# First MoE, chunks 2 to 8: high-weight products on high and low rows at once, halves added by DVE

## The chip, the cores and the metric

The kernel runs on one core of a Trainium2 chip. The metric is device time in microseconds of one execution. Its engines are PE (matrix products), PEld (PE's weight loads, shown apart), DVE (vector), ACT (scalar), POOL and SP (which issues loads).

## The reference

Three stages follow one another. Masked attention over 4 batches of 576 rows with 8 heads of 64 gives 2304 rows of 512. The first MoE normalises each row and adds a two-layer product:

```
xn = (x - mu) / np.sqrt(var + 1e-06) * g_ln
ch = np.maximum(xn @ w_ch1, 0.0) @ w_ch2     # w_ch1 512x2048, w_ch2 2048x512, fp32
return x + ch
```

The second MoE routes each row to one of 8 experts of hidden width 1024, again with a Relu between two products, and scales by the gate's probability.

## The kernel before, in words

Rows are worked in 9 chunks of CT = 256, numbered 0 to 8, kept transposed (model dimension on partitions). Every fp32 product is made of three products of a faster type: a value is split into a high part and the low rest, and high x high, high x low and low x high are summed in PSUM. `ln_split` (lines 620, 621) makes the split rows xc of a chunk: `xc[:, 0]` high (ACT), `xc[:, 1]` low (DVE), each 4 pieces of 256 columns. `w1t[f // 2]` holds the first weights with high at index 0 and low at index 1.

A tile is (c, f): chunk c and hidden block f of 128 units, 16 blocks to a chunk. `mm1(c, f)` sums 12 matmuls of 256 columns (4 pieces d by three terms) in the first half of a PSUM tile `ps_h`, of which there are two (tag "m"):

```
terms = [(d, a, b_) for d in range(4) for a, b_ in ((0, 0), (0, 1), (1, 0))]
for i, (d, a, b_) in enumerate(terms):
    pe.matmul(ps, w[:, a, d, o:o + 128], xcs[c][:, b_, d, :], ...)
act.activation(h[:, 0, :], ps, AF.Relu)
dve.scalar_tensor_tensor(h[:, 1, :], ps, 0.0, f32(h[:, 0, :]), op0=ALU.max, op1=ALU.subtract)
```

So ACT makes the high part of h (line 639, Relu), then DVE its low part (line 640). `mm2(c, f)` (line 653) multiplies h by the second weights, 12 matmuls into two PSUM tiles `acc` that sum over the 16 blocks. Its first matmul reads h's high part, its second the low part. `post` (lines 657, 658) then scales by the row's factor and adds to x.

The main loop walks over the tiles in `order`: chunks 0 and 1 interleaved, then chunks 2 to 8 block by block. At each it emits mm1 of this tile, and then mm2 of the tile before (`products`); at block 0 of a chunk from 2 on, the last block's mm2 comes first, ahead of the new chunk's mm1. Between them it emits side work: attention of batches 1 to 3 (lines 280 to 411, spread up to chunk 5), the next chunk's LayerNorm (lines 523 to 626), the routing of the chunk before (lines 673 to 764: `rt_rows` reads its products `ps_x` with ACT at line 675 and DVE at lines 676 and 677; the scans are at lines 717 and 718), and in chunk 8 the split of the first expert's weights (ACT line 780, DVE line 783) and its first rows (lines 873 to 897).

Each engine runs its instructions in one fixed order. That order isn't the source's: in this part the planner that builds the program takes, for each engine, whatever it models as ready at that time, the earliest in the source first, with durations of its own model. Waits between engines are put in by it as well. The pool `ln_p` holds one buffer of each tag.

Of the kernel before, what the change touches and what calls it, by code (L numbers as in the profile page):

```python
# [9 lines left out]
F32 = mybir.dt.float32  # L10
# [6 lines left out]
ALU = mybir.AluOpType  # L17
# [11 lines left out]
CT = 256  # L29
NCHUNK = NT // CT  # L30
# [27 lines left out]
ORDER = "TBXAMONF"  # L58

KA, NSURE = 4, 14  # L60


SMALL = 64
# [9 lines left out]
def attention_moe_moe(ctx: ExitStack, tc: tile.TileContext, q, k, v, g_ln, w_ch1, w_ch2, w_gate, w_local, w1, w2, out):  # L73
# [15 lines left out]
    pe, act, dve = Pin(nc.tensor), Pin(nc.scalar), Pin(nc.vector)  # L89
    pool, sp = nc.gpsimd, nc.sync  # L90

    def f32(ap):
        return ap.bitcast(F32)
# [19 lines left out]
    for j in range(2):  # L113
        m = mask_loc[64 * j:64 * j + 64, :]
        pool.affine_select(out=m, in_=m, pattern=[[-1, 128]], compare_op=ALU.is_ge, fill=-NEG, base=STR, channel_multiplier=1)
        pool.affine_select(out=m, in_=m, pattern=[[1, 128]], compare_op=ALU.is_ge, fill=-NEG, base=-1, channel_multiplier=-1)
        m = mask_str[64 * j:64 * j + 64]
# [35 lines left out]
    ln_p = ctx.enter_context(tc.tile_pool(name="ln_p", bufs=1))  # L153
    rt_p = ctx.enter_context(tc.tile_pool(name="rt_p", bufs=1))
    ps_acc = ctx.enter_context(tc.tile_pool(name="ps_acc", bufs=1, space=PSUM))
    ps_m = ctx.enter_context(tc.tile_pool(name="ps_m", bufs=2, space=PSUM))
# [22 lines left out]
    def side_r(shape, name):  # L179
        return ps_s["r"].tile(shape, F32, tag="s", name=name)  # L180
# [337 lines left out]
    lns, mus, xcs = {}, {}, {}  # L518
# [110 lines left out]

    def mm1(c, f):  # L630
        w, o = w1t[f // 2], (f % 2) * 128
        ps = ps_m.tile([128, 512], F32, tag="m", name="ps_h")[:, 0:CT]
        terms = [(d, a, b_) for d in range(4) for a, b_ in ((0, 0), (0, 1), (1, 0))]
        if c == 0:
            terms.sort(key=lambda t: t[1])
        for i, (d, a, b_) in enumerate(terms):
            pe.matmul(ps, w[:, a, d, o:o + 128], xcs[c][:, b_, d, :], start=(i == 0), stop=(i == 11))  # L637
        h = h_p.tile([128, 2, CT], F32R, tag="h", name="h")
        act.activation(h[:, 0, :], ps, AF.Relu)  # L639
        dve.scalar_tensor_tensor(h[:, 1, :], ps, 0.0, f32(h[:, 0, :]), op0=ALU.max, op1=ALU.subtract)  # L640
        hs[c, f] = h
# [322 lines left out]
    for n in range(2):  # L964
        i = n * (NE + 129)
# [97 lines left out]
    for t, (c, f) in enumerate(order):  # L1063
# [3 lines left out]
        if f == 0 and c > 1:  # L1067
# [6 lines left out]
            elif c == NCHUNK - 1:  # L1074
                load_turn(0)
                m2_p = ctx.enter_context(tc.tile_pool(name="m2_p", bufs=1))
        mm1(c, f)
        while late:
            post(late.pop(), 1)
# [31 lines left out]
    c = NCHUNK - 1  # L1111
# [39 lines left out]
    ps = side_r([1, 2, NE], "ps_n")  # L1151
# [86 lines left out]
    ps = side_r([128, NTILE], "ps_li")  # L1238
# [372 lines left out]
```

## Time and profile before

| what | value |
|---|---|
| median of 3 runs | 879.38 us (879.37 to 880.01) |
| profiled execution | 880.44 us, span 878.7 us |
| mean granted clock of PE | 0.992 |
| busy: PE, PEld, DVE, ACT, POOL | 850.7, 755.2, 470.5, 354.1, 152.4 us |
| first MoE, chunks 2 to 8 | about 195 to 604 us of the span |

Times in the rows below are from the span's start. Matmuls are pipelined: the duration of one is longer than the distance to the next one's start, and a merged row's length is from the first start to the last end. Idle time is what an engine stood still ahead of an instruction, with what released it.

### The profile page before, as it was taken

How to read it: one execution, taken by the hardware profiler on the slowest of the kernel's cores; microseconds unless marked ns; L12 is line 12 of the kernel's file. 1: busy time of each engine (PE TensorE's matmuls, PEld its weight loads, DVE VectorE, ACT ScalarE, POOL GpSimd, SP SyncE). 2: the span in 40 equal slices, each digit the busy share in tenths (PEclk: the TensorE clock that was granted, in tenths of full speed). 3: DMA queues.
4: the chain of work that ended last, by engine and by line, in shares of the span. 5: the costliest groups of instructions: out<-in, count | busy, mean ns of one | idle time of the engine just before them, and what ended most of it. 6: DMA issues, size and time to landing. Idle time of an engine off the chain costs nothing. (4 is left out here: it accounts for less than half of the span.)

```text
span 878.7 us, 18791 instructions
## 1 busy us (share of the span) xinstructions
PE 850.7 (97%) x7130; PEld 755.2 (86%) x7130; DVE 470.5 (54%) x1542; ACT 354.1 (40%) x857; POOL 152.4 (17%) x161
## 2 busy tenths in 40 slices
PE   9999899999999999999999999999989999999995
PEld 5678788889999999899999999999778877778774
DVE  4877766648666546655555464585824251121641
ACT  3687877642454233354221222242112252232651
POOL 2123332221120120120111212010031221111101
PEclk9999999999999999999999999999999999999998
DMA  9935342311212102210000000501265266445740
GB/s 182 264 116 182 110 143 45 89 38 52 67 41 47 49 2 55 53 37 20 25 1 25 1 26 1 193 29 47 92 226 203 94 225 249 144 146 210 268 150 23
DMA packets 96545, 87.15 MB, mean 99 GB/s; under 512 B 67378, under 2 KB 75574, under 8 KB 96440
## 3 DMA queue, kind: packets, MB, share of 16 engines
q1 hardware_dynamic: 89256, 69.61, 26.2%
q0 software_dynamic: 3552, 11.11, 3.8%
q10 hardware_dynamic: 3632, 5.09, 1.6%
q8 instruction: 59, 0.97, 0.5%
q14 instruction: 46, 0.38, 0.1%
HBM read 76.27 MB, written 9.97 MB: 98 GB/s over the span
## 5 line engine op out<-in xcount | busy, mean ns | idle before, releaser
L653 PE MATMUL acc<-h,w 128*128 128x256 f32 x1728 | 245.7, 290 | 3.4 <-DVE h L640 1.9
L637 PE MATMUL ps_h<-xc,w 128*128 128x256 f32 x1728 | 237.2, 286 | 0.1
L653 PEld LDWEIGHTS acc<-h,w 128*128 128x128 f32 x1728 | 218.3, 191 | 9.6 <-DVE h L640 3.6
L637 PEld LDWEIGHTS ps_h<-xc,w 128*128 128x128 f32 x1728 | 219.3, 192 | 2.2 <-DVE xc L621 0.5
L639 ACT ACTIVATE h<-ps_h 128x256 fp32r<-128x256 f32 x144 | 55.7, 388 | 214.6 <-PE ps_h L637 200.7
L640 DVE SCALAR_TENSOR_TENSOR h<-ps_h,h 128x256 fp32r<-128x256 f32 x144 | 60.6, 421 | 98.9 <-ACT h L639 98.4
L87 PE MATMUL ps_y<-wx,ht 128*128 128x512 f32 x336 | 83.6, 398 | 0.0
L87 PE MATMUL ps_h<-wx,xs 128*128 128x512 f32 x336 | 81.0, 397 | 0.0
L87 PEld LDWEIGHTS ps_h<-wx,xs 128*128 128x128 f32 x336 | 62.7, 188 | 14.8
L87 PEld LDWEIGHTS ps_y<-wx,ht 128*128 128x128 f32 x336 | 61.1, 188 | 11.9 <-issue 0.2
L482 POOL TENSOR_TENSOR w<-stg,w 128x512 fp32r<-128x512 f32 x32 | 44.0, 1374 | 125.6 <-ACT w L481 76.5
L1462 DVE TENSOR_TENSOR ht<-ps_th,ht 128x512 fp32r<-128x512 f32 x28 | 18.2, 686 | 39.4 <-ACT ht L1461 39.1
L1448 ACT ACTIVATE h<-ps_h 128x512 f32<-128x512 f32 x28 | 15.2, 595 | 57.8 <-PE ps_h L87 57.8
L783 DVE TENSOR_TENSOR wx<-raw,wx 128x1024 fp32r<-128x1024 f32 x32 | 37.3, 1220 | 1.3 <-ACT wx L780 1.3
L461 ACT ACTIVATE stg<-stg 128x512 f16<-128x512 f32 x27 | 37.2, 1377 | 0.0
L780 ACT CAST wx<-raw 128x1024 fp32r<-128x1024 f32 x32 | 31.8, 1057 | 5.7 <-PE acc L653 4.1
L355 ACT ACTIVATE sm<-sm,st 128x54 f32<-128x54 f32 (+1 forms) x80 | 27.6, 347 | 13.2 <-DVE st L343 13.2
L1486 POOL DMA_INDIRECT out_dram<-y,idx x14 | 18.5, 1323 | 77.5 <-ACT y L1485 57.9
L1461 ACT CAST ht<-ps_th 128x512 fp32r<-128x512 f32 x28 | 15.1, 589 | 35.6 <-PE ps_th L87 35.6
L1124 PE MATMUL ps_h2t<-x,wx 128*128 128x256 f32 x192 | 26.7, 297 | 2.7 <-DVE h2t L1129 2.7
L1124 PEld LDWEIGHTS ps_h2t<-x,wx 128*128 128x128 f32 x192 | 25.1, 202 | 3.1 <-DVE h2t L1129 2.9
L1485 ACT ACTIVATE y<-ps_y,pr 128x512 f32<-128x512 f32 x18 | 12.4, 688 | 34.2 <-PE ps_y L1475 16.8
(397 smaller groups left out, 1178.7 us busy)
## 6 DMA issues: line engine op xcount, KB each, us to landing
raws<-in_moe_w_dram SPq DMA_DIRECT2D x20, 1024.0 KB
stg<-in_moe_w_ch_dram SPq DMA_DIRECT2D x32, 512.0 KB
raw<-in_moe_w_dram SPq DMA_DIRECT2D x16, 1024.0 KB
xrows<-row ACTq DMA_DIRECT2D x9, 520.0 KB
qnat<-in_q_dram SPq DMA_DIRECT2D x48, 72.0 KB
knat<-in_k_dram SPq DMA_DIRECT2D x48, 72.0 KB
v<-in_v_dram SPq DMA_DIRECT2D x24, 72.0 KB
v<-in_v_dram SPq DMA_DIRECT2D x72, 18.0 KB
```

Source lines behind the costliest of these rows:

```text
L87: return lambda *args, **kw: tc.keep_in_program_order(fn(*args, **kw))
L355: act.activation(sm[0:m, i, :], (ps if mode else sm)[0:m, i, :], AF.Exp, bias=st[0:m, 0, i:i + 1], scale=-1.0, **({} if mode else dict(acc ...
L461: keep(act.activation(t.bitcast(F16)[..., 1], f32(t[..., 1]), AF.Copy, scale=2.0 ** -112))
L482: keep(pool.tensor_tensor(w[:, 1], r, f32(w[:, 0]), op=ALU.subtract))
L637: pe.matmul(ps, w[:, a, d, o:o + 128], xcs[c][:, b_, d, :], start=(i == 0), stop=(i == 11))
L639: act.activation(h[:, 0, :], ps, AF.Relu)
L640: dve.scalar_tensor_tensor(h[:, 1, :], ps, 0.0, f32(h[:, 0, :]), op0=ALU.max, op1=ALU.subtract)
L653: pe.matmul(accs[c][d // 2][:, d % 2, :], w[:, a, f % 2, d * 128:(d + 1) * 128], h[:, b_, :], start=(f == 0 and (a, b_) == (0, 0) and d % ...
L780: act.copy(wx[i][:, 0, :], raw[i // 2][:, i % 2, :])
L783: dve.tensor_tensor(wx[i][:, 1, :], raw[i // 2][:, i % 2, :], f32(wx[i][:, 0, :]), op=ALU.subtract)
L1124: pe.matmul(ps[:, j, :], wx[d][:, b_, 128 * f:128 * f + 128], x[:, a, d, :], start=(d == 0 and (a, b_) == PASS[0]), stop=(d == 3 and (a, b ...
L1486: pool.indirect_dma_start(out=out, out_offset=bass.IndirectOffsetOnAxis(ap=places(s)[1], axis=0), in_=y, in_offset=None, bounds_check=NT - ...
```

## The change

In chunks 2 to 8 mm1 uses the whole PSUM tile of 512 columns. Four matmuls take a high weight piece as stationary operand and the high and the low rows of that piece as one moving operand of 512 columns: the first 256 columns of the PSUM tile then hold high x high, the last 256 high x low. Four matmuls of 256 columns add low x high to the first half. ACT copies the second half to a new SBUF tile `low` (tag "low" in `ln_p`), DVE adds it to the first half in PSUM, and the Relu and the low half go on from there as before. Chunks 0 and 1 stay as they were.

```
+BOTH = range(2, NCHUNK)
     def mm1(c, f):
         w, o = w1t[f // 2], (f % 2) * 128
-        ps = ps_m.tile([128, 512], F32, tag="m", name="ps_h")[:, 0:CT]
+        ps = ps_m.tile([128, 512], F32, tag="m", name="ps_h")
+        if c in BOTH:
+            for d in range(4):
+                pe.matmul(ps, w[:, 0, d, o:o + 128], xcs[c][:, :, d, :], start=(d == 0), stop=False)
+            for d in range(4):
+                pe.matmul(ps[:, 0:CT], w[:, 1, d, o:o + 128], xcs[c][:, 0, d, :], start=False, stop=(d == 3))
+            low = ln_p.tile([128, CT], F32, tag="low", name="low")
+            act.copy(low, ps[:, CT:2 * CT])
+            dve.tensor_tensor(ps[:, 0:CT], ps[:, 0:CT], low, op=ALU.add)
+        ps = ps[:, 0:CT]
         terms = [(d, a, b_) for d in range(4) for a, b_ in ((0, 0), (0, 1), (1, 0))]
         if c == 0:
             terms.sort(key=lambda t: t[1])
-        for i, (d, a, b_) in enumerate(terms):
+        for i, (d, a, b_) in enumerate(() if c in BOTH else terms):
             pe.matmul(ps, w[:, a, d, o:o + 128], xcs[c][:, b_, d, :], start=(i == 0), stop=(i == 11))
```

## Rows read from the trace of the kernel before

**Rows 1.** The page's engine table: busy us (share of the span) xinstructions.

```profile
PE 850.7 (97%) x7130; PEld 755.2 (86%) x7130; DVE 470.5 (54%) x1542; ACT 354.1 (40%) x857; POOL 152.4 (17%) x161
```

**Rows 2.** Chunk 2, 7, most of 8: stretch, its length, each engine's busy us, clock.

```profile
195.00:250.00 55.00, 55.00 (x533) 52.20 (x532) 42.06 (x189) 21.85 (x80) 6.51 (x7) 1.00 0.19 51
...
500.90:551.30 50.40, 50.40 (x420) 49.63 (x419) 28.07 (x95) 11.28 (x30) 7.33 (x7) 1.00 0.03 12
...
568.00:592.00 24.00, 23.92 (x196) 22.75 (x195) 20.00 (x65) 10.17 (x17) 2.04 (x1) 1.00 0.18 64
```

**Rows 3.** Groups, 195 to 604 us: count | busy us, mean ns | idle before.

```profile
L637 PE MATMUL ps_h<-xc,w 128*128 128x256 f32 x1344 | 182.0, 284 | 0.0
```

**Rows 4.** Waits, 195 to 604 us, PE and weight loads: us, times, longest.

```profile
PE acc L653 <- DVE h L640: 0.7, 1, 0.7
...
PEld acc L653 <- DVE h L640: 1.1, 2, 0.9
```

**Rows 5.** Timeline, end of chunk 5: start us, us, engine, line, operation [idle before].

```profile
443.49 1.60 PE L637 MATMUL ps_h<-xc,w 128*128 128x256 f32 x12
...
444.93 1.60 PE L653 MATMUL acc<-h,w 128*128 128x256 f32 x12
445.13 0.38 ACT L639 ACTIVATE h<-ps_h 128x256 fp32r<-128x256 f32 x1 [2.50 <-PE ps_h L637]
445.55 0.42 DVE L640 SCALAR_TENSOR_TENSOR h<-ps_h,h 128x256 fp32r<-128x256 f32 x1 [2.46 <-ACT h L639]
...
447.81 3.04 PE L653 MATMUL acc<-h,w 128*128 128x256 f32 x24
...
448.43 0.42 DVE L640 SCALAR_TENSOR_TENSOR h<-ps_h,h 128x256 fp32r<-128x256 f32 x1 [2.46 <-ACT h L639]
...
452.75 0.42 DVE L640 SCALAR_TENSOR_TENSOR h<-ps_h,h 128x256 fp32r<-128x256 f32 x1
...
453.81 0.94 PE L653 MATMUL acc<-h,w 128*128 128x256 f32 x5
```

**Rows 6.** Timeline of PE, second MoE: two cuts of products with 512 columns.

```profile
864.84 3.34 PE L87 MATMUL ps_y<-wx,ht 128*128 128x512 f32 x14
...
774.78 3.42 PE L87 MATMUL ps_h<-wx,xs 128*128 128x512 f32 x14
```

**Rows 7.** Groups, 195 to 604 us: an ACT copy and a DVE product.

```profile
L675 ACT COPY row<-ps_x 128x256 f32<-128x256 f32 x32 | 11.9, 370 | 11.5 <-PE ps_x L673 10.5
L657 DVE TENSOR_TENSOR acc<-acc,rsb 128x512 f32<-128x512 f32 x16 | 11.2, 699 | 7.3 <-PE acc L653 7.1
```

**Rows 8.** Timeline, chunk 2: ACT and DVE read the same PSUM tile.

```profile
201.60 0.37 ACT L675 COPY row<-ps_x 128x256 f32<-128x256 f32 x1 [1.27 <-PE ps_x L673]
...
202.01 0.17 DVE L676 COPY lp<-ps_x 128x9 f32<-128x9 f32 x1 [1.19 <-ACT row L675]
```

**Rows 9.** Timeline, block 12 of chunk 7.

```profile
538.37 1.60 PE L637 MATMUL ps_h<-xc,w 128*128 128x256 f32 x12
...
540.70 0.36 ACT L639 ACTIVATE h<-ps_h 128x256 fp32r<-128x256 f32 x1
...
541.43 0.41 DVE L640 SCALAR_TENSOR_TENSOR h<-ps_h,h 128x256 fp32r<-128x256 f32 x1
...
542.69 0.52 PE L653 MATMUL acc<-h,w 128*128 128x256 f32 x3
```

**Rows 10.** Timeline, blocks 7 and 13 of chunk 8.

```profile
574.34 0.38 ACT L639 ACTIVATE h<-ps_h 128x256 fp32r<-128x256 f32 x1
...
577.30 0.42 DVE L640 SCALAR_TENSOR_TENSOR h<-ps_h,h 128x256 fp32r<-128x256 f32 x1
...
577.77 1.36 PEld L653 LDWEIGHTS acc<-h,w 128*128 128x128 f32 x11 [0.22 <-DVE h L640]
...
597.34 0.42 DVE L640 SCALAR_TENSOR_TENSOR h<-ps_h,h 128x256 fp32r<-128x256 f32 x1
...
597.81 0.86 PE L653 MATMUL acc<-h,w 128*128 128x256 f32 x5 [0.71 <-DVE h L640]
```

## The prediction

> **What bounds the kernel now.** I read the page's engine table first, then busy time by stretch, then the groups of the stretch that the diff touches, then who waited there, and last the timeline. The engine table says PE is busy for 97% of the span [rows 1]. The stretches say that this holds without a gap where the diff works: chunks 2 to 8 of the first MoE run from about 195 to 604 us, and in chunk 7 PE is busy 50.40 of 50.40 us at a granted clock of 1.00, while DVE works 28.07 and ACT 11.28 [rows 2]. The first product has 1344 matmuls of 256 columns there, 12 for each of 112 tiles (7 chunks by 16 hidden blocks), with 0.0 us of idle time before them [rows 3]. Waits of PE and its weight loads for the activated block h add up to 1.8 us in all of it [rows 4]. So PE's own time bounds this stretch: what is saved per matmul is saved in the end, and what h comes late, PE pays.
>
> How much later h may come is in the timeline [rows 5]. In a plain tick mm1 starts at 443.49, its last matmul ends at 445.09, ACT's Relu runs from 445.13 to 445.51, DVE's low half from 445.55 to 445.97. The second product that reads this h starts at 447.81 and reads the low half with its second matmul, at 447.93: 1.96 us of margin. Two places have less. The last block of a chunk has no first product between its own and its second product: h is done at 448.85, the second products of the two last blocks stand as one run from 447.81, and the later one's second matmul is at 447.81 + 13 x 0.12 = 449.37, margin 0.52. That pattern stands in chunks 3, 5, 6 and 7; in 2, 4 and 8 other PE work lies between. The first block of a chunk has DVE done at 453.17, the second product from 453.81 and its second matmul 0.31 later: 0.95, in chunks 6 to 8 (1.3 and more in the others).
>
> **What is saved on PE.** A 256-column matmul starts every (444.93 - 443.49) / 12 = 0.120 us [rows 5]. The change replaces four pairs of these per tile, on the same high weights, by four of 512 columns; four of 256 stay. The trace has 512-column products with the same kind of operands in the second MoE: fourteen in 3.34 us, the last 0.39 long, (3.34 - 0.39) / 13 = 0.227 each, and in another run (3.42 - 0.40) / 13 = 0.232 [rows 6]. Against 0.240 for a pair that is 8 to 13 ns, 31 to 53 ns per tile, 3.5 to 6.0 us over 112 tiles. No row has a moving operand in two pieces of 256 (high and low rows lie apart), nor a run as short as four; bounds are 0.240 (nothing saved) and 0.227 (6.0 us). I take 0.230, nearer the two rows than the bound: 40 ns per tile, **4.5 us saved**.
>
> The Trainium skill (TensorE: Matmul & The Clock Gate, Back-to-back issue gap) counts 262 cycles for 256 columns and 518 for 512, a fixed cost of about 2.5 ns per matmul. By that a merged pair gives back 2.5 ns and the change 4 x 112 x 2.5 ns = 1.1 us, an estimate from that page, not 4.5. The trace disagrees: 0.120 us is 13 ns over 256 columns at 2.4 GHz [rows 5].
>
> **What is added.** Per tile an ACT copy of 128x256 from PSUM and a DVE add with input and output in PSUM. For the copy the row is ACT's `row` copy of the same size, 0.37 us; for the add the ends are half of DVE's 512-column product in PSUM, 0.35, and the present low-half instruction, 0.42 [rows 5, 7]; I take 0.42, which has the same width. In engine time that is 112 x 0.37 = 41 us of ACT and 112 x 0.42 = 47 us of DVE over 409 us, where both have room on average: chunk 7 goes to (28.07 + 6.7) / 50.4 = 69% on DVE and 34% on ACT. Relu, low half, their buffers and all DMAs stay; the four high-on-low products move ahead of the low-weight ones, which changes nothing but that the first matmul now reads the low rows at once, done long before.
>
> In latency the chain from the last matmul to h becomes copy, add, Relu, low half: later by 0.04 + 0.37 + 0.04 + 0.42 = **0.87 us**, the 0.04 being the hand-overs of [rows 5]. If the copy could run beside the four low-weight matmuls, whose columns it does not read, it would be 0.46. I don't count on that: the trace has DVE's 9-column read of ps_x start at 202.01, 0.03 after ACT's read of other columns of the same tile ended, after 1.19 us of idle time [rows 8], so two engines are kept from one PSUM tile at a time.
>
> On ACT the added copy stands before Relu, and Relu then waits for DVE: behind it queue the next tile's copy, the LayerNorm's squares and scalings, and the casts of expert weights, and whatever the planner puts between copy and Relu delays Relu. On DVE the add waits for ACT, and behind it stand the routing and LayerNorm steps.
>
> **Where PE then waits.** Plain ticks keep 1.96 - 0.87 - 0.05 (the next first product is shorter) = 1.0 us. The rest:
> - Last blocks of chunks 3, 5, 6, 7: 0.87 - 0.52 = 0.35 each, 1.4 in sum; 0 if the planner runs the next chunk's first product meanwhile (its PSUM buffer is free). I take 0.7.
> - First blocks of chunks 6 to 8: 0.87 against 0.95, less what the DVE work queued there costs: 0.3 in sum, ends 0 and 1.
> - Tick 12 of chunks 3, 5, 6, 7, where LayerNorm of the next chunk is split: mm1 ends at 539.97, but Relu starts only at 540.70 behind squares and scalings, h is done at 541.84, needed at 542.81: margin 0.97 [rows 9]. With two more hand-overs in the same queues I get about 0.2 over the margin each: 0.8; ends 0 and 4.2 (one more 0.49 and one more 0.67 us instruction ahead each time).
> - The last chunk from 568 to 592: DVE already works 20.00 of 24.00 us [rows 2], eight adds make it 23.4. Two ticks have no margin today: Relu is done at 574.72, but the low half starts at 577.30 and PE's weight load goes on at 577.77; and the low half of 597.34 holds PE until 597.81 for 0.7 us [rows 10]. One add more ahead of each is 0.4, and once more an expert-weight subtraction of 1.2: I take 1.3; ends -1.0 (the new order removes both waits) and 5.
> - Chunk 2, DVE at 42.06 of 55.00 [rows 2], 89% with the adds, and the routing scans of chunks 3 to 7: 0.5; ends 0 and 3.
> Sum 0.7 + 0.3 + 0.8 + 1.3 + 0.5 = **3.6 us** given back. Net 4.5 - 3.6 = **0.9 us faster**. The profiled execution took 880.44 us (span 878.7), so 879.5 on its terms; it lies 1.06 above the median of the runs shown, 879.38, and against that the same sum is 878.5.
>
> **Rivals.**
> - *PE saves and h stays hidden.* The planner fills the waits, or the copy does start early (0.46 instead of 0.87, which fits under every margin of 0.52 and more). Then 4.5 us stay: 874.9. For it: margins of 2 to 5 us in most ticks of chunks 2 to 5, where attention work lies between. Against it: [rows 8 to 10].
> - *The queues decide.* ACT and DVE each do two steps of the chain and are in order; in the last chunk DVE is at 98%, so each late add delays the expert-weight subtraction behind it, and that the next low half. Place: 568 to 600 us and tick 12; price: 4 us there and 1 us in each of four tick-12 places, 8 in all with the rest as above at 1.5 gives 4 + 4 + 1.5 - 4.5 = +5.0: 884.4, slower. It decides from the point where a second instruction of 0.5 us or more stands between add and low half in more than half of those ticks.
> - *The pair is hardly shorter.* The 0.120 us between two starts need not hold a cost per matmul; if a moving operand in two pieces streams like two matmuls, a pair stays at 0.240, nothing is saved, and the waits remain: +3.6, 883.0, slower. For it: no row shows such an operand. Against it: contiguous 512 columns gain in both runs [rows 6]. The rule of the Trainium skill quoted above (TensorE: Matmul & The Clock Gate, Back-to-back issue gap) belongs here: with its 1.1 us saved the sum would be +2.5, an estimate.
>
> **How the numbers follow.** A measurement can tell about 0.2%, 1.76 us. Near balance (876.5 to 881.3): 0.42. PE saves: 0.27. Queues decide: 0.24. Pair hardly shorter: 0.07. Faster by over 1.76 us is below 877.6: all of the second and a quarter of the first, 0.37. Slower is above 881.1: the last two and a little of the first, 0.32. Same: 0.31. The likeliest case gives 878.5. The range takes in the second case's 874.9 with a saving at the 0.227 end (6.0 us: 873.4) and the queues up to 885.0.
>
> **What will show it.** Starts of the new 512-column products: 0.227 to 0.232 apart is right, 0.240 kills the saving. PE's waits for h in 195 to 604 us: 1.8 now, about 5 expected; near 2 means rival one, over 9 rival two. The gap between ACT's copy start and the tile's last matmul tells whether 0.87 or 0.46 holds. In the windows DVE from 568 to 592 should near 24 of 24. The forecast is wrong if PE has other new idle time than for h, if DVE's add takes far over 0.42, or if the second MoE from 604 us on changes its length.

## The result, and the profile after

The changed kernel takes 884.0 us (median of 6 runs, 882.68 to 885.95) beside 879.25 us for the kernel before (6 runs, 878.70 to 880.01): ratio 1.0052, interval 1.0035 to 1.0069. It is slower by 4.75 us, where 0.9 us faster was forecast; the time lies inside the range and beside the rival "the queues decide" (884.4). The profiled execution took 885.95 us (span 884.1), 2 us above its median; part of that is time at a lower granted clock, told in the last section.

The engine table of the page after (busy us, share, instructions) answers to [rows 1]:

```profile
PE 851.5 (96%) x6675; PEld 732.9 (83%) x6682; DVE 509.0 (58%) x1654; ACT 391.1 (44%) x969; POOL 152.4 (17%) x161
```

DVE grew by 38.5 us, ACT by 37.0; that is less than the new instructions' own 47.9 and 41.6 us below, since time that two records of one engine share counts once here. PE's busy time did not fall; its stretches at half clock, told below, count as busy. The groups of 195 to 610 us (count | busy us, mean ns | idle before), against [rows 3] and the forecast's instructions:

```profile
L636 PE MATMUL ps_h<-xc,w 128*128 128x512 f32 x448 | 125.8, 399 | 0.0
L663 PE MATMUL acc<-h,w 128*128 128x256 f32 x1364 | 194.9, 290 | 5.0 <-DVE h L650 5.0
...
L640 ACT COPY low<-ps_h 128x256 f32<-128x256 f32 x112 | 41.6, 371 | 145.8 <-PE ps_h L638 141.5 <-DVE nk L719 2.7 <-PE ps_li L773 1.1
L641 DVE TENSOR_TENSOR ps_h<-ps_h,low 128x256 f32<-128x256 f32 x112 | 47.9, 428 | 55.7 <-ACT low L640 54.5
```

The copy (371 ns) and the add (428 ns) cost what was assumed, 0.37 and 0.42 us. Of ACT's 145.8 us of idle time ahead of the copy 141.5 are for the products and none of the named rest is for the add, so it isn't the single buffer of `low` that holds the copy up. New is the idle time on the second product, L663: 5.0 us, all for DVE's low half of h. The waits of the same stretch (us, times, longest) against [rows 4]:

```profile
PEld acc L663 <- DVE h L650: 7.3, 12, 2.0
...
PE acc L663 <- DVE h L650: 5.0, 8, 1.8
```

Counted as in [rows 4] that is 12.3 us instead of 1.8; "over 9" was to mean the queues. Now a plain tick (a first product and the second product of another tile, with no side work between) and the end of chunk 6, timeline of after (start us, us, engine, line, operation [idle before]), against [rows 5]:

```profile
493.89 1.09 PE L636 MATMUL ps_h<-xc,w 128*128 128x512 f32 x4
...
494.82 0.63 PE L638 MATMUL ps_h<-xc,w 128*128 128x256 f32 x4
495.29 1.60 PE L663 MATMUL acc<-h,w 128*128 128x256 f32 x12
495.55 0.37 ACT L640 COPY low<-ps_h 128x256 f32<-128x256 f32 x1 [2.13 <-PE ps_h L638]
495.95 0.43 DVE L641 TENSOR_TENSOR ps_h<-ps_h,low 128x256 f32<-128x256 f32 x1 [2.08 <-ACT low L640]
496.42 0.38 ACT L649 ACTIVATE h<-ps_h 128x256 fp32r<-128x256 f32 x1 [0.50 <-DVE ps_h L641]
496.83 0.42 DVE L650 SCALAR_TENSOR_TENSOR h<-ps_h,h 128x256 fp32r<-128x256 f32 x1 [0.45 <-ACT h L649]
...
498.13 2.06 PE L663 MATMUL acc<-h,w 128*128 128x256 f32 x14
...
500.03 0.39 PE L636 MATMUL ps_h<-xc,w 128*128 128x512 f32 x1
500.26 1.35 PE L663 MATMUL acc<-h,w 128*128 128x256 f32 x10
```

Two things are to be seen. First product to second product is 495.29 - 493.89 = 1.40 us, before 444.93 - 443.49 = 1.44: the 40 ns per tile of the forecast. The four 512-column starts are (494.82 - 493.89) / 4 = 0.2325 us apart, a little above the 0.230 of the forecast, and the four low-weight ones (495.29 - 494.82) / 4 = 0.1175 instead of 0.120: about 30 ns of the 40 come from the pairs and 10 from the low-weight products. The chain, from the last matmul's end (495.45) to the end of the low half (497.25), is 1.80 us; before it was 445.97 - 445.09 = 0.88. So it grew by 0.92, forecast 0.87. The copy starts after all eight matmuls, not after the first four. At the chunk's end PE puts a matmul of the next chunk's first product (500.03) between the second products of the last block, and still loses time there.

Where the time went is read from the length of each chunk: from the start of its first second product to that of the next chunk (for chunk 8, to the start of its last matmul). For chunk 7 that is 556.46 - 504.34 = 52.12 us in after, and 550.70 - 500.86 = 49.84 in the run e1 below, which leaves copy and add out:

```profile
504.34 1.93 PE L663 MATMUL acc<-h,w 128*128 128x256 f32 x12
...
556.46 1.79 PE L663 MATMUL acc<-h,w 128*128 128x256 f32 x11
```

(after), and e1, whose second product has line 660:

```profile
500.86 1.78 PE L660 MATMUL acc<-h,w 128*128 128x256 f32 x12
...
550.70 1.54 PE L660 MATMUL acc<-h,w 128*128 128x256 f32 x10
```

All of them, in us, from the profiled executions (e3 and e5 are told below):

| chunk | 2 | 3 | 4 | 5 | 6 | 7 | 8 | 2 to 7 |
|---|---|---|---|---|---|---|---|---|
| before | 67.79 | 58.48 | 67.31 | 57.92 | 50.17 | 50.47 | 49.85 | 352.14 |
| after | 67.20 | 59.07 | 66.38 | 58.15 | 51.70 | 52.12 | 53.61 | 354.62 |
| e1 | 67.20 | 58.31 | 67.03 | 57.30 | 49.53 | 49.84 | 48.47 | 349.21 |
| e3 | 67.20 | 59.08 | 66.97 | 58.15 | 51.65 | 52.10 | 49.75 | 355.15 |
| e5 | 67.05 | 58.00 | 67.36 | 57.32 | 49.61 | 49.92 | 51.39 | 349.26 |

Chunks 2 and 4, with attention work between their products, keep the saving; chunks 3, 5, 6, 7 and 8 lose more than it against e1. Inside these chunks the losses stand at three kinds of place, got by comparing the end of each block's second product in after and in e1.

*The routing block*, block 6 of chunks 6 and 7: 1.03 and 1.15 us, with 0.14 and 0.15 more at block 5. Chunk 7, after:

```profile
520.24 0.63 PE L638 MATMUL ps_h<-xc,w 128*128 128x256 f32 x4
...
521.27 0.37 ACTq L710 DMA_DIRECT2D xrows<-row  x1
521.68 0.37 ACT L640 COPY low<-ps_h 128x256 f32<-128x256 f32 x1 [1.35 <-DVE nk L719]
...
522.60 0.74 DVE L727 TENSOR_TENSOR_SCAN oo<-nk,carry,d 8x256 f32<-8x256 f32 x1
523.26 0.40 DVE L641 TENSOR_TENSOR ps_h<-ps_h,low 128x256 f32<-128x256 f32 x1
523.58 1.18 DVE L728 TENSOR_TENSOR_SCAN d<-oo,carry 8x256 f32<-8x256 f32 x1
523.69 0.38 ACT L649 ACTIVATE h<-ps_h 128x256 fp32r<-128x256 f32 x1 [1.64 <-DVE ps_h L641]
...
524.73 0.40 DVE L650 SCALAR_TENSOR_TENSOR h<-ps_h,h 128x256 fp32r<-128x256 f32 x1
...
525.19 0.98 PE L663 MATMUL acc<-h,w 128*128 128x256 f32 x6 [0.56 <-DVE h L650]
```

The matmuls end at 520.87. The copy is ready then, but on ACT's queue stands the issue of the store of the routing rows, which waits for DVE; the copy runs at 521.68. On DVE the planner has put routing steps and the first scan ahead of the add, which runs at 523.26, and the second scan ahead of the low half, which runs at 524.73. The chain takes 525.13 - 520.87 = 4.26 us instead of 1.80: two steps on each of two in-order queues, each step behind other work.

*The LayerNorm block*, block 12 of chunks 3, 5, 6 and 7: 0.54 to 0.55 us each. Chunk 6, after, against [rows 9]:

```profile
490.74 0.42 DVE L641 TENSOR_TENSOR ps_h<-ps_h,low 128x256 f32<-128x256 f32 x1
490.89 0.49 ACT L621 ACTIVATE xc<-xt,g_sb 128x256 fp32r<-128x256 f32 x1
...
491.29 0.36 ACT L649 ACTIVATE h<-ps_h 128x256 fp32r<-128x256 f32 x1
491.42 0.67 DVE L622 SCALAR_TENSOR_TENSOR xc<-xt,g_sb,xc 128x256 fp32r<-128x256 f32 x1 [0.26 <-ACT xc L621]
...
492.01 0.41 DVE L650 SCALAR_TENSOR_TENSOR h<-ps_h,h 128x256 fp32r<-128x256 f32 x1
...
492.48 0.74 PE L663 MATMUL acc<-h,w 128*128 128x256 f32 x4 [0.29 <-DVE h L650]
```

One more 0.49 us scaling (490.89) stands before Relu and one more 0.67 us step (491.42) before the low half: the pair that the forecast named as the far end of this term, at 4.2 us for the four; it cost 2.2. *The chunk's end*: 0.45 us in the last block of each of chunks 3, 5, 6 and 7, and nothing in the first block behind it.

*The last chunk*: 53.61 - 48.47 = 5.1 us. Its worst place, block 7, after, against [rows 10]:

```profile
577.98 0.38 ACT L649 ACTIVATE h<-ps_h 128x256 fp32r<-128x256 f32 x1 [0.28 <-DVE ps_h L641]
578.17 0.74 DVE L727 TENSOR_TENSOR_SCAN oo<-nk,carry,d 8x256 f32<-8x256 f32 x1
...
578.84 1.19 DVE L793 TENSOR_TENSOR wx<-raw,wx 128x1024 fp32r<-128x1024 f32 x1
...
579.96 0.73 DVE L728 TENSOR_TENSOR_SCAN d<-oo,carry 8x256 f32<-8x256 f32 x1
...
580.66 0.40 DVE L650 SCALAR_TENSOR_TENSOR h<-ps_h,h 128x256 fp32r<-128x256 f32 x1
...
581.12 0.74 PE L663 MATMUL acc<-h,w 128*128 128x256 f32 x4 [1.76 <-DVE h L650]
```

Relu is done at 578.36; the low half starts at 580.66, behind two scans and an expert-weight subtraction. And after that the clock falls. Windows of after (stretch, length, busy us of PE, PEld, DVE, ACT, POOL, granted clock):

```profile
568.00:592.00 24.00, 22.14 (x144) 19.40 (x142) 18.62 (x58) 10.58 (x20) 0.00 (x0) 0.93 0.25 89
...
575.60:582.00 6.40, 4.64 (x33) 4.07 (x32) 6.19 (x13) 2.15 (x5) 0.00 (x0) 1.00 0.24 86
...
579.40:582.60 3.20, 1.48 (x10) 1.30 (x11) 2.94 (x11) 0.58 (x2) 0.00 (x0) 1.00 0.00 0
582.70:586.00 3.30, 3.30 (x14) 2.92 (x13) 2.38 (x8) 1.04 (x1) 0.00 (x0) 0.50 0.00 0
```

PE was busy for 1.48 of 3.20 us, and in the next 3.30 us the granted clock is 0.50 (1.2 GHz instead of 2.4): 3.30 x 0.5 = 1.65 us lost on top of the wait. DVE from 568 to 592 is busy 18.62 us, less than the 20.00 of before. But that window holds the time in which PE stood still and ran slowly. In the 6.40 us around the worst place DVE is busy 6.19 us, and it was as full there before, 2 us earlier on the span:

```profile
573.60:580.00 6.40, 6.37 (x51) 6.00 (x51) 6.22 (x18) 2.99 (x5) 0.00 (x0) 1.00 0.22 83
```

Here the new add meets a DVE without free time.

### The profile page after: what moved, and what is told of

Its sections match the earlier page's. It is cut to its first block, busy times and chain, and to the rows that moved or that the text cites. A ratio compares the mean times of both kernels' runs of the same rounds, so it can differ in the third digit from the quotient of the medians.

```text
span 884.1 us, 18127 instructions
## 1 busy us (share of the span) xinstructions
PE 851.5 (96%) x6675; PEld 732.9 (83%) x6682; DVE 509.0 (58%) x1654; ACT 391.1 (44%) x969; POOL 152.4 (17%) x161
## 5 line engine op out<-in xcount | busy, mean ns | idle before, releaser
L663 PE MATMUL acc<-h,w 128*128 128x256 f32 x1728 | 250.9, 291 | 7.8 <-DVE h L650 6.2
L663 PEld LDWEIGHTS acc<-h,w 128*128 128x128 f32 x1728 | 220.1, 191 | 17.6 <-DVE h L650 9.7
L636 PE MATMUL ps_h<-xc,w 128*128 128x512 f32 x448 | 125.8, 399 | 0.0
L640 ACT COPY low<-ps_h 128x256 f32<-128x256 f32 x112 | 41.6, 371 | 145.8 <-PE ps_h L638 141.5
L636 PEld LDWEIGHTS ps_h<-xc,w 128*128 128x128 f32 x448 | 77.2, 191 | 10.3
L641 DVE TENSOR_TENSOR ps_h<-ps_h,low 128x256 f32<-128x256 f32 x112 | 47.9, 428 | 55.7 <-ACT low L640 54.5
L638 PEld LDWEIGHTS ps_h<-xc,w 128*128 128x128 f32 x448 | 69.6, 189 | 9.9
L638 PE MATMUL ps_h<-xc,w 128*128 128x256 f32 x448 | 73.6, 283 | 0.0
L647 PE MATMUL ps_h<-xc,w 128*128 128x256 f32 x384 | 54.3, 288 | 0.1
L647 PEld LDWEIGHTS ps_h<-xc,w 128*128 128x128 f32 x384 | 49.1, 192 | 1.3 <-DVE xc L622 0.5
```

The source lines that it names most:

```text
L636: pe.matmul(ps, w[:, 0, d, o:o + 128], xcs[c][:, :, d, :], start=(d == 0), stop=False)
L638: pe.matmul(ps[:, 0:CT], w[:, 1, d, o:o + 128], xcs[c][:, 0, d, :], start=False, stop=(d == 3))
L640: act.copy(low, ps[:, CT:2 * CT])
L641: dve.tensor_tensor(ps[:, 0:CT], ps[:, 0:CT], low, op=ALU.add)
L663: pe.matmul(accs[c][d // 2][:, d % 2, :], w[:, a, f % 2, d * 128:(d + 1) * 128], h[:, b_, :], start=(f == 0 and (a, b_) == (0, 0) and d % ...
```

## Experiments

In the expectations Q is the theory that I formed on this profile: the pairs save what was forecast, and the longer chain to h, held up in the queues of ACT and DVE, costs PE twice that. Any other letter is the rival of that one experiment.

**e1: the saving without the chain.** Copy and add are left out, so the product of the high weights with the low rows is missing from the sum.

```diff
-            low = ln_p.tile([128, CT], F32, tag="low", name="low")
-            act.copy(low, ps[:, CT:2 * CT])
-            dve.tensor_tensor(ps[:, 0:CT], ps[:, 0:CT], low, op=ALU.add)
```

> Leaves out the copy and the add, so the high x low half is computed on PE but never added; the chain to h is Relu and low half as before the change. Theory Q (PE saves 40 ns in each of 112 tiles, and the longer chain through the queues of ACT and DVE gives back about twice that): 879.3 - 4.5 = 874.8 us, between 873.5 and 876, and PE's waits for h in chunks 2 to 8 back near 1.8 us. Rival P (the merged product itself saves little, or costs PE in another way): 878 or more.

Measured 874.69 us (6 runs, 873.24 to 876.31) beside 879.37: 0.9953 [0.9939, 0.9968], 4.7 us faster. Forecast for the saving: 4.5. The Trainium skill (TensorE: Matmul & The Clock Gate, Back-to-back issue gap) would have it at 1.1, the estimate in the prediction; the measurement decides against it. So copy and add cost 884.0 - 874.7 = 9.3 us in this kernel, where 3.6 were forecast.

**e2: the chain without the saving.** The products stay at 256 columns, twelve per tile, but high on low goes to the second half as in the change, with copy and add.

```diff
-                pe.matmul(ps, w[:, 0, d, o:o + 128], xcs[c][:, :, d, :], start=(d == 0), stop=False)
+                for b_ in range(2):
+                    pe.matmul(ps[:, CT * b_:CT * b_ + CT], w[:, 0, d, o:o + 128], xcs[c][:, b_, d, :], start=(d == 0 and b_ == 0), stop=False)
```

> Twelve 256-column products as before the change, high x low into the second half of the PSUM tile, then copy and add as in the change: the chain alone. Theory Q: the change without its saving, 884.0 + 4.5 = 888.5 us, between 887 and 890. Rival P (what costs is the merged product and its operand in two pieces, the chain is mostly hidden): 880 to 883.

Measured 890.49 us (4 runs, 889.80 to 891.89): 1.0131 [1.0117, 1.0146], 11.1 us slower, 0.5 above the range that I gave and far from the rival's 880 to 883. Its profile has two stretches of half clock in chunk 8 (at 584 and 608 us; the chunk runs from 559 to 616). The two halves of the change, -4.7 and +11.1, add up to +6.4 where the whole shows +4.75: the sum holds to 1.7 us, about one such stretch.

**e3: all but the last chunk.**

```diff
-BOTH = range(2, NCHUNK)
+BOTH = range(2, NCHUNK - 1)
```

> The change in chunks 2 to 7 alone, chunk 8 as before. In the two profiles chunk 8 is 3.8 us longer after the change, with a fall of the granted clock in it. Theory Q: 884.0 - 3.8 = 880.2 us, between 879.3 and 881.2: the last chunk with its full DVE queue carries most of the loss, the six others are +2 in sum. Rival E (the loss is spread evenly, 0.7 us per chunk): 883.3.

Measured 882.46 us (5 runs, 880.74 to 883.31): 1.0037 [1.0024, 1.0050]. The expectation of Q (880.2) is missed by 2.3 us, the rival's 883.3 by 0.8. I had taken the last chunk's share from the profiled execution, with its clock fall; in medians that chunk carries 884.0 - 882.46 = 1.5 of the 4.75 us, and as the intervals of e3 and of the whole change overlap, even this 1.5 isn't clear of noise. The chunk table, too, puts much of the loss outside it: e3 loses 355.15 - 349.21 = 5.9 us in chunks 2 to 7 against e1. PE's waits for h in e3 from 195 to 610 us are seven, 2.8 us in sum, the longest 0.6.

**e8: the routing rows' store issued by SP instead of ACT**, in the changed kernel (from the second chunk on).

```diff
-        act.dma_start(xrows[c * CT:(c + 1) * CT, :].rearrange("(j p) e -> p j e", p=TT), r["row"])
+        (sp if c else act).dma_start(xrows[c * CT:(c + 1) * CT, :].rearrange("(j p) e -> p j e", p=TT), r["row"])
```

> The change, with the store of the routed rows issued on SP instead of ACT for chunks 1 to 8. After the change block 6 of chunks 6 and 7 is 1.2 us late each: the copy stands behind that issue, which waits for DVE, then the add behind a scan and the low half behind the next scan. Theory Q: with the copy free to start 0.8 us earlier, both wins: 884.0 - 2.0 = 882.0 us, block 6 without a wait of PE. Rival S (the scans on DVE alone hold the chain, the issue is only named last): 883.5 or more, and block 6 still 0.8 us late or more.

Measured 880.79 us (12 runs, 879.66 to 881.55) beside 879.63: 1.0016 [1.0007, 1.0025], against 1.0052 [1.0035, 1.0069] with the store on ACT. 0.36% is 3.2 us, more than the 2.0 that Q expected. Timeline of e8, the same block 6 of chunk 7:

```profile
518.93 0.63 PE L638 MATMUL ps_h<-xc,w 128*128 128x256 f32 x4
...
519.65 0.37 ACT L640 COPY low<-ps_h 128x256 f32<-128x256 f32 x1 [0.63 <-PE ps_h L638]
...
519.94 0.36 SPq L710 DMA_DIRECT2D xrows<-row  x1
...
520.40 0.43 DVE L641 TENSOR_TENSOR ps_h<-ps_h,low 128x256 f32<-128x256 f32 x1
...
521.28 0.42 DVE L650 SCALAR_TENSOR_TENSOR h<-ps_h,h 128x256 fp32r<-128x256 f32 x1
...
521.93 0.74 DVE L727 TENSOR_TENSOR_SCAN oo<-nk,carry,d 8x256 f32<-8x256 f32 x1
```

The copy runs 0.09 us after the matmuls, the add and the low half are through before the scans start, and the chain takes 521.70 - 519.56 = 2.14 us instead of 4.26. In the routing blocks of chunks 6 and 7 PE has no wait left, and only the 0.14 and 0.15 us of block 5 remain against e1; the losses at block 12 (0.55) and at the chunk ends (0.45) are as in after, and chunk 8 shows no clock fall in this execution. So one issue of 0.37 us in the wrong queue did about a third of the 9.3 us, together with the order that followed from it: with the issue on SP the planner also put the add and the low half ahead of both scans on DVE, and no run parts the two.

**e5: the change, with the second product two tiles behind the first** (from block 2 on, chunks 2 to 8), so that h has one more tick. If h is merely late, this takes the waits away; if ACT or DVE has no time left, it doesn't.

```diff
+        if c > 1 and f > 1:
+            products(1)
...
-    def products():
+    def products(keep=0):
-        while pend:
-            c, f = pend.pop()
+        while len(pend) > keep:
+            c, f = pend.pop(0)
...
-                products()
+                if not (c > 1 and f > 1):
+                    products()
```

> The change, with the second product of a tile put two tiles behind the first instead of one (from block 2 of each of the chunks 2 to 8; at a chunk's end both are emptied as now). The chain to h then has 4.2 us or more instead of 2.8. The copy, add, Relu and low half are all still there. Theory Q with latency as the cause: nearly all waits for h go, 874.8 to 876.5 us, faster than both kernels. Rival L (the cause is the amount of work on DVE and ACT, not how late h is): 881 or more, with DVE as the engine that PE waits for.

Measured 877.6 us (12 runs, 874.30 to 878.68) beside 879.37: 0.9973 [0.9962, 0.9984], faster than both. It is 1.1 us above the range expected. No second product waits for h any more; chunks 2 to 7 take 349.26 us, as in e1 (349.21), which has no copy and no add. What is left is in chunk 8, 51.39 beside 48.47. Timeline of e5 there:

```profile
573.85 1.20 DVE L795 TENSOR_TENSOR wx<-raw,wx 128x1024 fp32r<-128x1024 f32 x1
...
575.69 0.29 PE L740 MATMUL ps_oo<-iw,oo 40*128 40x40 f32 x2 [1.49 <-DVE oo L733]
```

and two windows of e5:

```profile
570.00:576.00 6.00, 4.48 (x34) 4.01 (x32) 5.89 (x13) 2.35 (x5) 0.00 (x0) 1.00 0.26 91
...
577.00:580.30 3.30, 3.30 (x17) 3.20 (x16) 2.36 (x10) 1.32 (x2) 0.00 (x0) 0.53 0.00 0
```

PE waits 1.49 us for the routing's `oo`, whose steps stand behind an expert-weight subtraction on DVE (busy 5.89 of the 6.00 us up to there), and then the clock is 0.53 for 3.30 us. So one more tick takes away the waits for h, but not the loss where DVE has no free time.

**e6: the lag alone, on the kernel before** (the diff of e5, without the change).

> The kernel before with the same second lag, no merged product, no copy, no add. Theory Q: before, PE waited only 1.8 us for h in chunks 2 to 8, so the lag alone gives at most that: 878.4 us, between 877.6 and 879.4, and the merged product is what the lagged version gains by. Rival G (the lag is a gain by itself): 877 or less, and the merged product then adds nothing to it.

Measured 879.95 us (12 runs, 877.90 to 880.94) beside 879.63: 1.0007 [0.9997, 1.0016], no difference that can be told. The lag gives nothing by itself; in e5 it gives back what the longer chain took in chunks 2 to 7.

**e7: e5 without the last chunk** (the diffs of e5 and e3 together).

> The lagged version of the change with chunk 8's first product as before (lagged, but not merged). In the lagged profile chunk 8 is 51.4 us long against 49.9 before, and PE waits 1.5 us there for the routing scan behind three weight subtractions on a full DVE. Theory Q: without 16 adds on that DVE the wait goes, while 0.6 us of saving go too: 877.6 - 1.0 = 876.6 us. Rival O (the wait comes from the order that the lag makes, whatever the adds): 878.2 or more.

Measured 877.03 us (10 runs, 875.59 to 878.79) beside 879.63: 0.9970 [0.9960, 0.9980]. That is nearer to Q's 876.6 than to the rival's 878.2, but e5's interval is nearly the same, so by their times e5 and e7 cannot be told apart. The trace goes with Q: without chunk 8's adds PE has no wait for `oo`, and chunk 8 shows no half clock. With e5 it is the fastest version that computes everything. What remains are two short waits of a first product for a PSUM tile that the low half still reads (1.1 us in sum; e6 has them too).

## Why the prediction was wrong

**The saving: right in its size.** 40 ns per tile, 4.7 us in e1 for 4.5. Its parts were a little off: the 512-column starts are 0.2325 apart instead of 0.230, and the low-weight products, forecast as unchanged, give the other 10 ns. That the two meet at 40 is luck.

**The instructions and the chain: right.** Copy 0.37, add 0.43, the chain longer by 0.92 instead of 0.87, no early copy. Outside chunks 2 to 8 the two profiled spans differ by little: (884.1 - 878.7) - (408.23 - 401.99) = -0.8 us.

**"Where PE then waits", sum 3.6 us: the step that failed.** 9.3 us in medians (884.0 - 874.7). By terms, from the profiled executions of after and e1:

| term | forecast | seen |
|---|---|---|
| last blocks | 0.7 | 4 x 0.45 = 1.8 |
| first blocks | 0.3 | 0 |
| tick 12 of chunks 3, 5, 6, 7 | 0.8 | 0.54 to 0.55 each, 2.2 |
| chunk 2 and routing scans | 0.5 | 1.17 and 1.30 in chunks 6 and 7, 2.5 |
| last chunk | 1.3 | 5.1, of which 1.65 half clock |

These add to 11.6; chunk 4 (-0.65) and -0.23 and -0.15 in chunks 3 and 5 take it to the 10.55 us by which the seven chunks of after are longer than those of e1. The chunks' sum is above the medians' 9.3; the profiled after has a clock fall in chunk 8, which by their mean clocks not every execution has.

What the terms have in common: I took the chain as 0.87 us longer and priced each place by the margin that it lacked. But a chain of four steps that changes engine three times joins an in-order queue four times. At a quiet place that costs the hand-over, 0.03 to 0.10 us; at a busy one other work stands ahead of each step, and a step that is late finds the next engine at other work too. In the routing block one 0.37 us issue ahead of the copy, itself waiting for DVE, and the scans ahead of add and low half became 2.46 us (4.26 - 1.80). I had given the routing scans of chunks 3 to 7 half a microsecond with no row behind it, and had not looked at what ACT issues there.

**"The queues decide": right in its mechanism, in size partly by luck, in place partly.** Its point of decision, an instruction of 0.5 us or more between add and low half, is met in 7 of its 12 ticks: block 12 of chunks 3, 5, 6 and 7 (0.67) and blocks 5, 7 and 11 of the eight of chunk 8 (in block 7 three: 0.74, 1.19, 0.73). Block 6 of chunks 6 and 7, which it did not name, has one of 1.18. Its prices were 4 for the last chunk, 4 for tick 12 and 1.5 for the rest; seen are 5.1, of which 1.65 half clock that it did not have, 2.2, and 3.2. So 884.4 met 884.0 by errors that offset each other. Outside chunk 8 stand 5.4 of the 10.55 us of the profiles, and 3.1 of the 4.75 in medians (e3). That in chunks 2 to 7 it is lateness and not engine time is shown by e5: with every copy, add, Relu and low half still there, one tick more of room takes away the waits for h. In chunk 8 DVE's time counts as well: it is full around the worst place, e5 still loses 2.9 us there, and e7, without that chunk's adds, has no such wait.

**Not settled.** Block 12 and the chunk ends were not changed one by one; that they are the same thing rests on the timeline, and on e5, which removes all of them together. In e8 the place of the issue and the order on DVE changed together. In e5 the three fastest runs are 874.30 to 874.93, at e1's level, with a mean granted clock of 0.995 or 0.996, and nine are 876.54 to 878.68 at 0.990 to 0.992: the nine spend more time at half clock. That the fall behind the wait in chunk 8 is part of it is seen in one profile alone.

## What to carry to other kernels

When a change swaps time on the bounding engine for steps in the chain that feeds it, price each new step at the places where its queue is busy: write down what stands in that in-order queue, DMA issues included, when the step becomes ready, since one late step makes the next one late. A chain that is late can be paid for with distance instead of speed: one more tile of lag gave the whole saving back outside the last chunk, and cost nothing by itself (e5, e6). An engine's busy share over a long window says little about this: DVE was busy 18.62 of 24.00 us around the place where PE lost most, and 6.19 of 6.40 in it.

## What the hardware showed that was not expected

A wait of TensorE can cost nearly twice its length, where the granted clock falls to 0.50 behind it: in after 1.76 us of waiting were followed by 1.65 us lost at half clock. The four 512-column products in that stretch take 1.91 us, four of the same in the plain tick above 1.09 (timeline of after):

```profile
583.00 1.91 PE L636 MATMUL ps_h<-xc,w 128*128 128x512 f32 x4
```

The same happens, or not, at one place of the second MoE that the change doesn't touch, where PE waits for DVE's h2t. There 24 products take 4.57 us in before, 4.65 in after and 3.14 in e1 (timelines of PE, of before and of e1):

```profile
645.61 4.57 PE L1124 MATMUL ps_h2t<-x,wx 128*128 128x256 f32 x24 [2.68 <-DVE h2t L1129]
```

```profile
639.91 3.14 PE L1131 MATMUL ps_h2t<-x,wx 128*128 128x256 f32 x24 [2.11 <-DVE h2t L1136]
```

That is 1.4 to 1.5 us. The wait ahead of it is 2.68 us in before and 2.20 in after; it is 2.11 in e1, and in e3 2.70 with 3.14 us for the products, so the length of the wait alone doesn't decide. Ahead of the kernel's last microseconds the profile of before has two stretches at half clock (at 92.5 and 645.5 us), that of after three (101.4, 582.7 and 650.9), those of e1 and e3 none. The two executions of after with a mean clock of 0.990 took 885.86 and 885.95 us, the four at 0.993 and 0.994 took 882.68 to 884.41. A comparison of two profiles by a few microseconds should count these stretches first.
